# Two more blocks of a fused DeltaNet and hard-swish MLP kernel with fewer multiplications: block one's product with w_out by seven, block three's product with w_in by eleven

## The chip, the cores and the metric

The kernel runs on one core of one Trainium2 chip. The core has five engines that run side by side, each with its own queue of instructions which it takes strictly in order: TensorE (PE in the profile; its weight loads are listed as PEld), VectorE (DVE), ScalarE (ACT), GpSimd (POOL) and SyncE (SP), which here issues nearly all DMAs. An instruction waits at the head of its queue until the semaphores that it names are reached, and everything behind it on that engine waits with it.

The metric is the device time of one execution in microseconds (us). Lower is better.

## The reference

The first half is a gated delta rule over 768 steps for 4 batches and 8 heads of width 48; the second half is a two-layer MLP on the result.

```python
k_n = k / (np.linalg.norm(k, axis=-1, keepdims=True) + 1e-06)
for t in range(S):                                   # 768 steps
    y[:, :, t] = q_t @ state
    v_old = state . k_t
    state += beta_t * outer(k_t, v_t - v_old)
x = y.transpose(0, 2, 1, 3).reshape(3072, 384)
h = x @ w_in                                         # 384 -> 2048
g = h * clip(h + 3, 0, 6) / 6
out = g @ w_out                                      # 2048 -> 384
```

All arrays are float32 but the two weights, which arrive as float64; they are loaded in 16 pieces of 768 KB and converted to float32 on the core.

## The kernel before, in words

**Attention in steps.** The 768 positions are cut into 24 steps of 32. One step t handles 32 positions of all four batches, so 128 rows. Three parts belong to a step:

- its *preparation* (`prep`): GpSimd scales the keys into `kb` (L510), TensorE transposes keys and queries (`pt`, L524), ScalarE copies them to `KQ` (L532), TensorE multiplies them (`sc`, L547), and VectorE masks the products into `L` and `LB` (L558), with masks `mb` that GpSimd makes (L486) and into which only one buffer is given, so a mask waits until VectorE has read the one before. GpSimd also makes `bkb` (L498);
- the *inverse* of the triangular matrices, taken for a group of four steps at once by VectorE in some 60 small instructions with two operands in SBUF (`pr`, `A`: L759, L764), between two large transposes (L469, L473);
- the *chain* of the step, which carries the state: `ks` (L806), `R` (L901, L909), `pz` (L827), `R` from `pz` (L927), `su` (L938), the state's update (L956), `py` (L827), `y` (L819, L863) and the transposition `yt` (L873, L877), which delivers 128 rows of the MLP's input.

Before the preparation of a group, the norms of its keys are needed (`norms`, L409 the square, L413 its sum, L417 to L431 the root and its inverse). For later groups GpSimd does the square, into one buffer, so that squares and sums take turns.

**MLP in blocks.** Two steps make one block of 256 rows, twelve blocks in all. For a block the kernel first makes g = act(x @ w_in) in 16 or 8 portions (*up*) and then g @ w_out (*down*). Both come in a plain form and in one with fewer multiplications:

- `up`: 16 portions of 3 products each, 128x256 (L994), then ScalarE (L1001) and VectorE (L1004);
- `up_by_eleven`: 8 portions, each with 7 products of 128 columns and 2 of 256 columns instead of 6 of 256 (L1066); it wants sums of the weights (`weight_sums`, 16 instructions of GpSimd, L1030), sums of the inputs (`token_sums`, VectorE, L1056), two additions of GpSimd on each portion (L1030) and more of ScalarE (L1080, L1100, L1110) and VectorE (L1093, L1097, L1113);
- `down`: 32 products of 384 columns (L1162), results copied by ScalarE (L1173);
- `down_by_seven`: Strassen's scheme in Winograd's form, 7 products of half width, that is 56 of 192 columns (L1226). Its operands are quarters of w_out (B11, B12, B21, B22) and differences of them (T1, T2, T4, and a last one that replaces B12), made by `quarters` and `last_quarter` (L1197, L1203); sums of g are made by VectorE (L1212) and sums of the results by GpSimd or VectorE (L1236).

Before the change, `FIRST = 2` means that blocks 2 to 11 go down by seven and blocks 0 and 1 plainly, and `UF = 4` means that blocks 4 to 11 go up by eleven and blocks 0 to 3 plainly.

**What sets the order.** The program up to step 5 is written out by hand as a string of words, `ORDER` (L21 and following), in which a word stands for one small piece: `k`, `q`, `v`, `w` for loads, `a` and `c` for the conversion of the weights (L356 on ScalarE; L378, L383, L389 on VectorE), `p9` for the next piece of step 9's preparation, `i2` for the next piece of group 2's inverse, `u` for the next unit of the MLP, and so on. From step 5 on a loop places the work: each step has 15 units; in each unit a piece of the chain or of a preparation is given out by a table (`plan`), one unit of the MLP follows, and pieces of the next group's inverse (`fill`) are added by a budget. Before the change steps 5 and 6 each carry two preparations (`behind`), and group 3's inverse begins at the start of step 7. The pieces of `rest` (conversions, then `quarters`) are given out one in a unit.

The buffers in PSUM are few: a ring of four banks (`pm`) holds `ph`, `po`, `pt`, `pz`, `py` and `yt`; a ring of two double banks (`pc`) holds `sc`, `ks` and `su`. A product of TensorE whose bank still has to be read by VectorE or ScalarE waits for that reader.

The functions that the change touches, with their callers:

Of the kernel before, what the change touches and what calls it, by code (L numbers as in the profile page):

```python
# [36 lines left out]
u h4 k*2 c q k*9 q u p8*2 x4 k ru k*2 gu k c n9 q u q*2 p8 k*2 b7 n9*2 i2 u x4 q i2*2 q ub ru gu u  # L37
rb gb i2*2 h4*2 u*2 i2 ru i2*6 y4 i2 gu i2*7 u i2 ru gu i2 u*3 ru i2*4 gu ru i2*2 v i2 c gu u*3 a u
ru c i2 u*2 i2 gu i2*3 q i2*5 y4 h4 n9 i2 e*2 n9*2 i2*4 q i2 y4 e n9 u ru i2*3 u i2 ru*2 gu h4 u n9
i2*2 u i2 e i2*6 y4 u k n9*3 u gu i2 y4 n9 i2 p9 q i2*2 gu  # L40
# [4 lines left out]
def kernel(  # L45
# [972 lines left out]
    UF = 4  # L1018
# [134 lines left out]
    def down(blk, c, f0):  # L1153
# [7 lines left out]
        for f in range(f0, f0 + WF):  # L1161
            nc.tensor.matmul(  # L1162
                pos[c][:], lhsT=gs[blk, f // 2][:, f % 2, c * P : (c + 1) * P], rhs=w_out[:, f, :],
                start=(f == 0), stop=(f == NFC - 1),
            )
        if f0 + WF == NFC:
# [19 lines left out]
    FIRST = 2  # L1186
# [6 lines left out]
    def quarters():  # L1193

        for o, a, b in ((T1, B12, B11), (T2, B22, T1), (T4, T2, B21)):
            for f in range(0, HF, 2):
                nc.vector.tensor_tensor(  # L1197
# [3 lines left out]

    def last_quarter(f):
        nc.vector.tensor_tensor(  # L1203
            out=B12[:, f : f + 2], in0=B22[:, f : f + 2], in1=B12[:, f : f + 2], op=ALU.subtract
        )

    def down_by_seven(blk):
# [32 lines left out]
        settle()  # L1240
# [56 lines left out]
    def mlp_units():  # L1297
# [21 lines left out]
        for blk in range(1, N // CB):  # L1319
# [82 lines left out]
    def early_norms(t):  # L1402
# [5 lines left out]
    rest = chained(convert(), quarters())  # L1408
    gens.update(
        a=scales(), c=rest, w=pieces(), q=queries(), v=values(), B=betas(), k=keys(), z=settings(), s=more_settings(),  # L1410
# [41 lines left out]
    with tc.manual_schedule():  # L1452
# [111 lines left out]
```

## Time and profile before

| | us |
|---|---|
| median of three executions | 664.48 (664.38 to 665.51) |
| the profiled execution | 662.4 |
| its span in the profile | 660.6 |
| TensorE busy | 633.3 |
| VectorE busy | 492.7 |
| ScalarE busy | 276.7 |
| GpSimd busy | 217.0 |

The profiled execution took 662.4 us, 1.8 us more than its span of 660.6 us. The profile gives the busy time of each engine, the chain of work that ended last, groups of equal instructions by line, and a timeline in which neighbouring instructions of one kind are merged into one row (start, duration, engine, line, operands, shape, count and, in brackets, idle time before it with its releaser). One float32 product of TensorE shows as two records, so a count of x16 stands for eight products. The granted TensorE clock was 0.982 of full speed on average; the stretches below full speed lie in the first 50 us.

The steps can be told from the rows of `ks` (L806) in the chain: step 5 starts at 152.66 us, step 6 at 179.95, step 7 at 207.31, step 8 at 232.91, step 9 at 258.71, step 10 at 283.92.

### The profile page before, as it was taken

What the parts mean: (1) busy time and instruction counts of PE and PEld (TensorE: products, weight loads), DVE (VectorE), ACT (ScalarE), POOL (GpSimd) and SP (SyncE); (2) the same over time, 40 slices, a digit from 0 to 9 for tenths busy, and PEclk for the clock granted to TensorE, in tenths of its full rate; (3) what the DMA queues carried; (4) which work ended last, traced back from release to release, by engine and by line L of the source; (5) the groups of instructions that cost most, each with busy time, mean ns of one, the idle gap of its engine ahead of it and who ended that gap; (6) DMA issues with size and microseconds to landing.
All of it is one profiled execution on the core that took longest, in us unless ns stands there. A gap on an engine that the chain in (4) does not pass through costs nothing.

```text
span 660.6 us, 26484 instructions
## 1 busy us (share of the span) xinstructions
PE 633.3 (96%) x11592; PEld 567.8 (86%) x11592; DVE 492.7 (75%) x1158; ACT 276.7 (42%) x540; POOL 217.0 (33%) x336
## 2 busy tenths in 40 slices
PE   2768999999999999999999999999999999999997
PEld 2657987776789989999999999999999999999997
DVE  5899877798546698758988848989658998456354
ACT  5897689331243142154144244244244144153250
POOL 6531122003411363553254354164052241331430
PEclk9759999999999999999999999999999999999999
DMA  7888246212140030032030030030020020010000
GB/s 178 209 230 201 76 102 164 45 27 42 27 85 3 12 65 3 2 74 38 2 75 2 3 74 2 3 63 3 2 50 2 2 50 2 14 27 1 26 1 24
DMA packets 88691, 33.27 MB, mean 50 GB/s; under 512 B 80224, under 2 KB 83424, under 8 KB 88576
## 3 DMA queue, kind: packets, MB, share of 16 engines
q1 hardware_dynamic: 88224, 31.29, 21.1%
q8 instruction: 91, 1.49, 0.9%
q10 hardware_dynamic: 352, 0.30, 0.2%
q14 instruction: 24, 0.20, 0.1%
HBM read 26.84 MB, written 4.72 MB: 48 GB/s over the span
## 4 chain that ended last, share of the span: by engine, by line
PE 92%; ACT 3%; DVE 2%; DMA 2%; SPq 1%; issue 0%; ACTq 0%; DVEq 0%
PE po L1226 28%; PE ph L1066 24%; PE ph L994 12%; PE po L1162 6%; PE ks L806 4%; PE pt L524 3%; PE py L827 3%; PE pz L827 3%; PE sc L547 3%; PE su L938 3%; ACT spare L356 2%; DMA kf<-in_k_dram 1%; PE yt L873 1%; PE pi L684 1%; DVE pr L730 1%; DVE A L735 0%
## 5 line engine op out<-in xcount | busy, mean ns | idle before, releaser
L1066 PE MATMUL ph<-xT,w_in 128*128 128x128 f32 (+1 forms) x640 | 139.0, 321 | 0.0
L1226 PE MATMUL po<-w_out,g 128*128 128x192 f32 x640 | 110.6, 326 | 0.0
L1066 PEld LDWEIGHTS ph<-xT,w_in 128*128 128x128 f32 x640 | 104.0, 191 | 5.9
L1030 POOL TENSOR_TENSOR g<-g 128x256 f32<-128x256 f32 (+1 forms) x128 | 78.3, 613 | 92.8 <-ACT g L1080 87.8
L1226 PEld LDWEIGHTS po<-w_out,g 128*128 128x128 f32 x640 | 104.6, 190 | 0.5
L994 PE MATMUL ph<-xT,w_in 128*128 128x256 f32 (+1 forms) x480 | 93.3, 343 | 1.5 <-DVE g L1004 1.0
L1226 PE MATMUL po<-spare,g 128*128 128x192 f32 x480 | 86.7, 332 | 0.0
L994 PEld LDWEIGHTS ph<-xT,w_in 128*128 128x128 f32 x480 | 76.2, 190 | 11.5 <-DVE g L1004 1.3
L1226 PEld LDWEIGHTS po<-spare,g 128*128 128x128 f32 x480 | 77.2, 190 | 1.8
L1080 ACT ACTIVATE g<-ph 128x512 f32<-128x512 f32 x64 | 38.2, 597 | 92.8 <-PE ph L1066 92.8
L1236 POOL TENSOR_TENSOR o<-o,u 128x192 f32<-128x192 f32 x18 | 13.7, 762 | 165.9 <-ACT o L1233 87.9
L759 DVE TENSOR_TENSOR pr<-A 128x30 f32<-128x30 f32 (+9 forms) x150 | 58.8, 392 | 3.1
L1093 DVE TENSOR_TENSOR g<-ph,g 128x256 f32<-128x256 f32 x64 | 26.8, 419 | 44.4 <-PE ph L1066 39.5
L1212 DVE TENSOR_TENSOR g<-g 128x512 f32<-128x512 f32 x80 | 56.3, 724 | 4.6 <-PE po L1226 4.5
L764 DVE TENSOR_TENSOR A<-A,pr 128x30 f32<-128x30 f32 (+9 forms) x150 | 56.0, 373 | 3.5
L1001 ACT ACTIVATE g<-ph,halves 128x256 f32<-128x256 f32 (+1 forms) x80 | 33.7, 428 | 56.7 <-PE ph L994 56.7
L356 ACT ACTIVATE spare<-spare,places 128x768 uint16<-128x768 uint16 (+1 forms) x56 | 52.5, 942 | 2.3 <-DMA kf<-in_k_dram 1.2
L1113 DVE SCALAR_TENSOR_TENSOR g<-o,g 128x512 f32<-128x512 f32 x64 | 46.4, 725 | 6.8 <-ACT o L1110 6.8
L1110 ACT ACTIVATE o<-g,halves 128x512 f32<-128x512 f32 x64 | 46.2, 723 | 10.5 <-DVE g L1113 7.8
L1066 PE MATMUL ph<-beta_tok,sums_in 128*128 128x128 f32 x256 | 49.5, 275 | 0.0
L1233 ACT ACTIVATE o<-po 128x192 f32<-128x192 f32 x40 | 13.2, 330 | 82.9 <-PE po L1226 79.3
L510 POOL TENSOR_TENSOR kb<-kf,inv 128x384 f32<-128x384 f32 x24 | 21.7, 905 | 74.0 <-issue 43.1
(141 smaller groups left out, 1022.0 us busy)
## 6 DMA issues: line engine op xcount, KB each, us to landing
kf<-in_k_dram SPq DMA_DIRECT2D x96, 48.0 KB, 2.5
qb<-in_q_dram SPq DMA_DIRECT2D x96, 48.0 KB, 2.7
vf<-in_v_dram SPq DMA_DIRECT2D x96, 48.0 KB, 2.0
out_dram<-o SPq DMA_DIRECT2D x90, 48.0 KB, 1.6
spare<-in_moe_w_in_dram SPq DMA_DIRECT2D x4, 768.0 KB, 5.3
w_out<-in_moe_w_in_dram SPq DMA_DIRECT2D x4, 768.0 KB, 5.6
w_out<-in_moe_w_out_dram SPq DMA_DIRECT2D x4, 768.0 KB, 7.4
spare<-in_moe_w_out_dram SPq DMA_DIRECT2D x4, 768.0 KB, 5.0
```

What stands on the lines that cost most here:

```text
L356: nc.scalar.activation(out=z, in_=z if n else d.bitcast(I16)[:, :, :, 3], func=func, bias=places[:, n : n + 1], scale=scale,)
L759: nc.vector.tensor_tensor(out=pv, in0=A[:, j + 1 :, j].unsqueeze(2).to_broadcast([n, w, j]), in1=A[:, j, 0:j].unsqueeze(1).to_broadcast([n ...
L764: nc.vector.tensor_tensor(out=A[:, j + 1 :, 0:j], in0=A[:, j + 1 :, 0:j], in1=pv, op=ALU.subtract)
L827: nc.tensor.matmul(ps[rows(place(b)), D * h : D * h + D], lhsT=m(h)[rows(b)], rhs=z[rows(b), D * at(h) : D * at(h) + D], start=True, stop= ...
L994: nc.tensor.matmul(ph[:, cols], lhsT=w_in[:, s, f * 128 : (f + 1) * 128], rhs=xT[:, s, cols], start=(s == 0), stop=(s == NKT - 1),)
L1030: nc.gpsimd.tensor_tensor(out=out, in0=a, in1=b, op=op)
L1066: nc.tensor.matmul(ph[:, n], lhsT=w, rhs=x, start=start, stop=stop, skip_group_check=True)
L1110: nc.scalar.activation(out=r, in_=g, func=ACTF.Relu, bias=half, scale=1.0 / 6.0)
L1113: nc.vector.scalar_tensor_tensor(out=g, in0=r, scalar=1.0, in1=g, op0=ALU.min, op1=ALU.mult)
L1162: nc.tensor.matmul(pos[c][:], lhsT=gs[blk, f // 2][:, f % 2, c * P : (c + 1) * P], rhs=w_out[:, f, :], start=(f == 0), stop=(f == NFC - 1),)
L1212: nc.vector.tensor_tensor(out=A(f, *out, 4), in0=A(f, *a, 4), in1=A(f, *b, 4), op=op)
L1226: nc.tensor.matmul(ps[n][:], lhsT=A(f - f % 2, *a)[:, f % 2], rhs=b[:, f], start=(f == 0), stop=(f == HF - 1),)
```

## The change

Block 1 goes down by seven (`FIRST = 1`), and block 3 goes up by eleven (`UF = 3`). So that the operands for block 1 are there in time, `quarters` now makes all four sets of differences, on GpSimd instead of VectorE, as 16 instructions (12 for T1, T2 and T4, 4 for the new B12) which the new words `t` place in `ORDER`: twelve after `b7`, four later. `last_quarter` and the place in `up(2)` that called it are gone, and the MLP's units no longer drain `rest` there. Since T2 and T4 need all of w_out, the last pieces of its conversion (two words `c`, one word `a`) come earlier, ahead of group 2's inverse. `ORDER` has two units `u` less at its end, because block 1's down now has 14 units instead of 16; the loop from step 5 on is thus at the same unit of the MLP as before.

In the loop, step 5 alone is `behind` and carries the preparations of steps 9, 10 and 11 (pieces in units 1 to 6, then 3 to 8, then 9 to 13), and the first piece of step 12's at its end. Step 6 has one preparation as all later steps, and group 3's inverse begins in unit 6 of step 6. The sums of w_in for the products by eleven are made in block 2's down instead of block 3's.

```diff
@@ ORDER
-u h4 k*2 c q k*9 q u p8*2 x4 k ru k*2 gu k c n9 q u q*2 p8 k*2 b7 n9*2 i2 u x4 q i2*2 q ub ru gu u
-rb gb i2*2 h4*2 u*2 i2 ru i2*6 y4 i2 gu i2*7 u i2 ru gu i2 u*3 ru i2*4 gu ru i2*2 v i2 c gu u*3 a u
-ru c i2 u*2 i2 gu i2*3 q i2*5 y4 h4 n9 i2 e*2 n9*2 i2*4 q i2 y4 e n9 u ru i2*3 u i2 ru*2 gu h4 u n9
-i2*2 u i2 e i2*6 y4 u k n9*3 u gu i2 y4 n9 i2 p9 q i2*2 gu
+u h4 k*2 c*3 q k*9 q u p8 a p8 x4 k ru k*2 gu c k n9 q u q*2 p8 k*2 b7 t*12 n9*2 i2 u x4 q i2*2 q ub
+ru gu u rb gb i2*2 h4*2 u*2 i2 ru i2*6 y4 i2 gu i2*7 u i2 ru gu i2 u*3 ru i2*4 gu ru i2*2 v i2 gu
+u*3 t*4 u ru i2 u*2 i2 gu i2*3 q i2*5 y4 h4 n9 i2 e*2 n9*2 i2*4 q i2 y4 e*2 n9 u ru i2*3 u i2 ru*2
+gu h4 u n9 i2*2 u i2*7 y4 k n9*3 gu i2 y4 n9 i2 p9 q i2*2 gu
...
-    UF = 4
+    UF = 3
...
-    FIRST = 2
+    FIRST = 1
...
     def quarters():
-        for o, a, b in ((T1, B12, B11), (T2, B22, T1), (T4, T2, B21)):
+        low = tuple(("low", c, f) for c in range(CB) for f in range(0, HF, WF))
+        for o, a, b, which in (
+            (T1, B12, B11, 14), (T2, B22, T1, 15), (T4, T2, B21, None), (B12, B22, B12, None)
+        ):
+            if which is None:
+                needs(("w", NW - 1), *(low if o is B12 else ()))
+            else:
+                needs(("seen", which, 0), ("seen", which, 1))
             for f in range(0, HF, 2):
-                nc.vector.tensor_tensor(
+                needs(("w", NWI + f // 2))
+                if o is not T1:
+                    needs(("w", NWI + (HF + f) // 2))
+                nc.gpsimd.tensor_tensor(
                     out=o[:, f : f + 2], in0=a[:, f : f + 2], in1=b[:, f : f + 2], op=ALU.subtract
                 )
                 yield
-
-    def last_quarter(f):
-        nc.vector.tensor_tensor(
-            out=B12[:, f : f + 2], in0=B22[:, f : f + 2], in1=B12[:, f : f + 2], op=ALU.subtract
-        )
...
-        settle()
+        if blk > FIRST:
+            settle()
...
-                for n, _ in enumerate((up_by_eleven if blk + 1 >= UF else up)(blk + 1)):
-                    if blk + 1 == FIRST and n >= HF:
-                        drain(rest)
-                        if n % 2:
-                            last_quarter(n - HF - 1)
-                    yield
+                yield from (up_by_eleven if blk + 1 >= UF else up)(blk + 1)
...
-            behind = t - LS < LA - LE
-            first_of = t + min(LA, LE + t - LS)
-            now, more, later = (prep_of(first_of + n) for n in range(3))
+            behind = t == LS
+            now, more, third, later = (prep_of(t + LA - n) for n in (2, 1, 0, -1))
             if not behind:
-                more, later = (), more
+                now = third
...
-                for u in (7, 8, 10, 11, 12, 13):
-                    plan[u] = lambda ch=plan.get(u): (ch and u < 13 and ch(), take(more))
-                plan[14] = lambda: take(later)
-            ready = (2, 0) if behind or i == 2 and t - LS == LA - LE else (1, 6)
+                plan[13] = None
+                for u, gen in zip((3, 5, 6, 7, 8, 9, 10, 11, 12, 13), (more,) * 5 + (third,) * 5):
+                    plan[u] = lambda old=plan.get(u), gen=gen, first=u == 8: (
+                        first and take(gen), old and old(), first or take(gen)
+                    )
+            ready = (1, 6)
...
+            if behind:
+                take(later)
```

More of the change, by code (lines that the diff above doesn't have):

```diff
@@ L1165, in down @@
             )
+        past.add(("low", c, f0))
         if f0 + WF == NFC:
@@ L1407 @@
     g_all = mlp.tile([128, NFC, TB], FP32, name="g", bufs=1)
-    rest = chained(convert(), quarters())
+    rest = convert()
     gens.update(
-        a=scales(), c=rest, w=pieces(), q=queries(), v=values(), B=betas(), k=keys(), z=settings(), s=more_settings(),
+        a=scales(), c=rest, w=pieces(), q=queries(), v=values(), B=betas(), k=keys(), z=settings(), s=more_settings(), t=quarters(),
         ua=up(0, 0), ub=up(0, 1), u=mlp_units(),
@@ L1497 @@
             if behind:
-                for u in (7, 8, 10, 11, 12, 13):
-                    plan[u] = lambda ch=plan.get(u): (ch and u < 13 and ch(), take(more))
-                plan[14] = lambda: take(later)
-            ready = (2, 0) if behind or i == 2 and t - LS == LA - LE else (1, 6)
+                plan[13] = None
[4 more added lines that the diff above has]
+            ready = (1, 6)
             for u in range(NU):
-                if u in plan:
+                if plan.get(u):
                     plan[u]()
```

## The prediction

> **What bounds the kernel now.** I read the page first, for the busy shares and the chain that ended last:
>
> ```profile
> PE 633.3 (96%) x11592; PEld 567.8 (86%) x11592; DVE 492.7 (75%) x1158; ACT 276.7 (42%) x540; POOL 217.0 (33%) x336
> PE 92%; ACT 3%; DVE 2%; DMA 2%; SPq 1%; issue 0%; ACTq 0%; DVEq 0%
> ```
>
> TensorE carries 92% of the chain. Busy time by stretches shows it at 10.00 of every 10 us from 70 to 200 us and within 0.04 us of full on to 600, and the waits of TensorE between 93 and 300 us are nil. So any product taken away there is time saved, and any new wait of TensorE is time lost, in full. The chain in order of time prices the products, plain and with fewer multiplications:
>
> ```profile
> 161.58 5.36 PE po L1162 x16
> ...
> 188.89 5.38 PE ph L994 x24
> ...
> 267.67 5.40 PE po L1226 x32
> ...
> 292.52 5.05 PE ph L1066 x36
> ```
>
> These are the four kinds, each for four units of MLP work. Next, who hands TensorE its work between 110 and 175 us, where the change rearranges everything. TensorE's timeline:
>
> ```profile
> 132.25 2.75 PE L994 MATMUL ph<-xT,w_in 128*128 128x256 f32 x12
> ...
> 147.01 2.74 PE L1162 MATMUL po<-w_out,g 128*128 128x384 f32 x8
> ...
> 155.07 0.60 PE L524 MATMUL pt<-ident,kb 128*128 128x128 f32 x4
> ...
> 160.72 0.86 PE L547 MATMUL sc<-KQ 64*32 64x64 f32 x64
> ...
> 166.87 0.89 PE L938 MATMUL su<-R,bkb 32*64 32x48 f32 x64
> ```
>
> VectorE's and GpSimd's timelines:
>
> ```profile
> 110.10 1.47 DVE L389 SCALAR_TENSOR_TENSOR w_out<-spare 128x768 f32<-128x768 f32 x1
> ...
> 120.59 0.42 DVE L1004 SCALAR_TENSOR_TENSOR g<-g,ph 128x256 f32<-128x256 f32 x1 [1.26 <-ACT g L1001]
> ...
> 132.67 0.41 DVE L1004 SCALAR_TENSOR_TENSOR g<-g,ph 128x256 f32<-128x256 f32 x1
> ...
> 134.27 0.40 DVE L764 TENSOR_TENSOR A<-A,pr 128x228 f32<-128x228 f32 x1
> ...
> 139.43 0.42 DVE L1004 SCALAR_TENSOR_TENSOR g<-g,ph 128x256 f32<-128x256 f32 x1
> ...
> 153.35 0.34 DVE L431 RECIPROCAL inv<-nt 128x32 f32<-128x32 f32 x1
> ...
> 235.14 0.81 DVE L764 TENSOR_TENSOR A<-A,pr 128x228 f32<-128x228 f32 x1
> ```
>
> ```profile
> 108.42 2.33 POOL L498 TENSOR_TENSOR bkb<-kb,beta_tok 128x384 f32<-128x384 f32 x2
> ...
> 153.83 0.83 POOL L510 TENSOR_TENSOR kb<-kf,inv 128x384 f32<-128x384 f32 x1 [43.08 <-issue]
> ...
> 271.28 1.20 POOL L409 TENSOR_TENSOR sq<-kf 128x384 f32<-128x384 f32 x1 [0.67 <-DVE ss L413]
> 273.15 1.20 POOL L409 TENSOR_TENSOR sq<-kf 128x384 f32<-128x384 f32 x1 [0.66 <-DVE ss L413]
> ```
>
> The reader is to see three things. VectorE has no idle time between 121 and 154 us: it works at group 2's inverse and TensorE lives on a margin of tenths. The same instruction (L764, 228 elements) takes 0.40 us with GpSimd still and 0.81 us while GpSimd works. And GpSimd's idle 43 us before 153.83, where the new differences go, is the very time in which VectorE has none.
>
> **What is saved.** *Down of block 1:* its nine pieces of L1162 in the chain sum to 21.24 us; block 2's seven pieces by seven (L1226, the same steps' interruptions) sum to 18.80. Saved: 2.4 us. *Up of block 3:* 21.32 us (L994, from 229 us) against 20.07 for block 4 (L1066): 1.3 us; steps 7 and 8 together last 51.4 us, steps 9 and 10 50.0, which agrees. Together -3.7 us, all on the path.
>
> **What is hidden.** The twelve quarter sums leave VectorE in step 5 (0.54 to 0.85 us each) and the eight sums of block 1 (L1212, 0.68 free) come in; TensorE waited for neither. The last four (L1203) leave up(2). The 16 sums of w_in move one block earlier on GpSimd; in steps 8 and 9 of before they ran beside the plain up(3) and an inverse with no wait of TensorE, and they meet the same there now; without that cover each would cost its 0.8 us. Block 3's extra work for VectorE (token sums 2.0 us a block, L1093, L1097, L1113 11.5 against 6.6) and ScalarE (12.8 against 6.8) meets an inverse that starts nine units sooner, as in steps 10 to 12, which keep TensorE full. SyncE's loads keep their places; the outputs of block 1 now wait for the end of its product, as every later block's do. Preparation 11 moves from step 6 to 5 with all its instructions: the same 1.7 us of TensorE (two `pt` of 0.43, one `sc` of 0.8), elsewhere.
>
> **Wait C: VectorE falls behind under the new differences.** In its queue the last conversion (L383, L389: 2 x 0.95 us) now stands before the inverse. 1.26 us of it fit in the idle time before 120.59; with that the queue is 0.6 us late. GpSimd may start T2 when that L383 ends, near 120.9, and then has T2, T4 and the new B12 back to back: twelve instructions of 128x384, 0.83 us each (L510 free). The first six meet L389 (once, +0.5) and then instructions that read PSUM or one operand, which the rows show unharmed (L558 0.41, L413 0.55, L469 1.97 in either case); the other six meet the inverse's first pairs. What does one cost VectorE? The nearest row is the L389 at 110.10 beside the second 128x384 `bkb`: 1.47 against 0.95, +0.52. So 0.6 + 0.5 + 6 x 0.52 = 4.2, less 0.5 for two L1004 that run underneath: 3.7 us late near 133 us. TensorE's second half of the row at 132.25 (from 133.55) needs the bank that the L1004 at 132.67 frees, at 133.08: slack 0.5. TensorE waits about 3.2 us, wherever on the way it comes. Ends: GpSimd's 128x256 sums cost 0.29 each (two rounds of the inverse from 234.19 to 237.56 last 3.37 instead of 2.18, beside four of them), giving 1.8 us; 0.83 each, full exclusion, gives 5.1. I take 0.52 since that row has instructions of the same size. A gain is excluded, since TensorE waits for nothing there today.
>
> [...]
>
> **Wait D: the keys of step 9 come too late.** After 139 us VectorE works without a gap from the L1004 at 139.43, which follows TensorE's own portion, to the reciprocal at 153.35, whose result `kb` needs (L510, 153.83 to 154.66). None of that gets shorter; the conversions left before 139.43. TensorE's `pt` is at 155.07, 0.4 later. But between 147.01 and that `pt` TensorE now has three half products by seven (24 records, 3.9 us) instead of 20 plain records (6.6 us): it arrives 2.7 us sooner and waits 2.3. C shifts both alike. Ends: 0.4 if VectorE could use the 1.9 us of the conversions, 2.7 if `kb` also slips.
>
> **Wait E: three preparations in step 5.** `sc` of step 10 now stands three units after step 9's, before `su`, and `su` needs its second double bank back: VectorE must have made `LB` of step 10. In VectorE's queue that L558 stands behind three sums L413 of the norms, each waiting for a GpSimd square. GpSimd's queue holds, before the first square, step 10's mask, which waits for step 9's `LB`. From the end of step 9's `sc`: `LB` +0.8, two masks 1.2 to 1.6, one addition 0.6 to 0.8, then three rounds of square and sum at 1.87 (271.28 to 273.15) less a little for the first, L558 twice 0.75: about 9. TensorE gets there after four half products (5.2), two transposes (0.9) and `sc` (0.8): 6.9. Wait 2.0; ends 0.5 (squares at 0.83 free) and 2.6.
>
> **Sum.** -3.7 + 3.2 + 2.3 + 2.0 = +3.8 us. Against the profiled execution of 662.4 us (span 660.6 and 1.8 around it, which stay): 666.2. That execution lies 2.1 us under the median of the three, 664.48; on that median the sum gives 668.3.
>
> **Rivals.** *Full exclusion* (condition: each of the six differences costs VectorE its 0.83): C is 5.1, the sum +5.7, 670.2 us. *E does not bite* (GpSimd's squares free of VectorE's sums, so the rounds take 1.4): E 0.5, sum +2.3, 666.8 us. For it: in step 5 of before squares followed at 1.8 to 2.5 us, not faster, so little. [...]
>
> **How the numbers follow.** Main case 0.55, full exclusion 0.13, no E 0.17, ahead 0.10, a mixture within the bound 0.05. What a measurement of this kernel can tell from no change is 0.2%, 1.3 us. The first three are slower by more: 0.85; faster 0.10; same 0.05. The low ends of C, D and E together give -1.0 us (663.5), the high ends +6.7 (671.2). The range, 663.2 to 671.2, holds these and leaves out the faster case.
>
> **What would show it.** L1162 halves to 64 records; block 1's L1226 lasts 18.8 us. TensorE's waits, nil now between 93 and 300 us, show VectorE's L1004 near 130 to 137, GpSimd's `kb` at step 5's first `pt`, and VectorE's L558 at step 5's `su`. L759 and L764 right after L469 show 0.5 to 0.9 us instead of 0.2. From step 7 on every step lasts 25 us. If the waits are not there, I am wrong in the queues; if they are and the sum differs, in a price.

## The result, and the profile after

The changed kernel is slower: 674.5 us (median of six executions, 670.3 to 677.6) against 664.2 us for the kernel before on the same chip, a ratio of 1.0146 with a 95% interval of 1.0105 to 1.0188. Measured again it was 675.5 us, ratio 1.0137 (1.0097 to 1.0177). The forecast was 668.3 us. Its sign holds, its size does not: +3.8 us were forecast, about +10 came, and the time lies above the range.

The page of the changed kernel, busy shares and then the chain that ended last:

```profile
PE 631.5 (94%) x11688; PEld 575.3 (86%) x11688; DVE 502.6 (75%) x1164; ACT 282.2 (42%) x551; POOL 243.7 (36%) x373
...
PE 83%; issue 6%; DVE 4%; DMA 3%; POOL 2%; ACT 1%; SPq 1%; POOLq 0%; DVEq 0%
```

TensorE is busy for 1.8 us less than before, in a span that is 11.5 us longer (672.1 against 660.6; the execution took 673.81 us). Its share of the chain fell from 92% to 83%, and "issue", time for which the profile shows no releaser, rose from 0% to 6%. Most of that 6% is no wait of TensorE: 25.7 us of it are GpSimd's idle time from the end of its last difference (136.67 us) to the next `kb` (162.44), along which the chain is followed. What TensorE itself lost is in its timeline. It shows the new waits, in brackets with their releaser; before the change there was none from 93 to 300 us:

```profile
130.35 0.88 PE L827 MATMUL pz<-R,X 32*32 32x48 f32 x64 [1.00 <-DVE g L1004]
...
138.76 1.56 PE L994 MATMUL ph<-xT,w_in 128*128 128x256 f32 x6 [2.15 <-DVE g L1004]
142.09 1.56 PE L994 MATMUL ph<-xT,w_in 128*128 128x256 f32 x6 [1.77 <-DVE g L1004]
...
163.36 0.66 PE L524 MATMUL pt<-ident,kb 128*128 128x128 f32 x4 [2.04 <-POOL kb L510]
...
178.93 0.84 PE L938 MATMUL su<-R,bkb 32*64 32x48 f32 x60 [1.47 <-DVE LB L558]
...
277.51 0.30 PE L547 MATMUL sc<-KQ 64*32 64x64 f32 x2 [0.96 <-issue]
...
479.44 1.78 PE L1232 MATMUL po<-spare,g 128*128 128x192 f32 x10 [0.87 <-issue]
```

The first three are wait C (4.9 us together), then D (2.0) and E (1.5), in the places that the prediction named. The last two were in no step of it. VectorE and GpSimd under C:

```profile
120.12 0.74 DVE L901 SCALAR_TENSOR_TENSOR R<-ks,parity,vf 128x192 f32<-128x192 f32 x2 [1.72 <-ACT y L843]
...
129.05 0.94 DVE L764 TENSOR_TENSOR A<-A,pr 128x30 f32<-128x30 f32 x1
...
130.99 0.92 DVE L764 TENSOR_TENSOR A<-A,pr 128x58 f32<-128x58 f32 x1
131.94 0.94 DVE L759 TENSOR_TENSOR pr<-A 128x84 f32<-128x84 f32 x1
132.92 0.93 DVE L764 TENSOR_TENSOR A<-A,pr 128x84 f32<-128x84 f32 x1
...
136.85 0.29 DVE L764 TENSOR_TENSOR A<-A,pr 128x130 f32<-128x130 f32 x1
```

```profile
116.94 3.88 POOL L1208 TENSOR_TENSOR spare<-w_out 128x384 f32<-128x384 f32 x4 [3.06 <-ACT spare L356]
124.27 4.71 POOL L1208 TENSOR_TENSOR spare<-w_out,spare 128x384 f32<-128x384 f32 x4 [3.45 <-DVE spare L383]
128.93 3.85 POOL L1208 TENSOR_TENSOR spare<-spare,w_out 128x384 f32<-128x384 f32 x4
132.75 3.92 POOL L1208 TENSOR_TENSOR w_out<-w_out 128x384 f32<-128x384 f32 x4
```

While GpSimd worked here, VectorE finished one two-operand instruction for each of GpSimd's: GpSimd's came every 0.96 us, and six of VectorE's, of 30 to 108 elements, lasted 0.92 to 0.95. From 136.85 on, with GpSimd still, 130 elements took 0.29. The pace was GpSimd's own: its four differences from 116.94 on came at the same distance (3.88 us for four), although VectorE was idle among them for 1.72 us, up to 120.12. So in this stretch VectorE alone was held up; only the first difference, at 124.27, had itself waited, beside an L389 of VectorE.

The kernel before shows the same one for one where GpSimd makes sums of w_in beside an inverse. Each of VectorE's instructions ends 0.25 us after one of GpSimd's:

```profile
236.20 0.59 DVE L759 TENSOR_TENSOR pr<-A 128x234 f32<-128x234 f32 x1
236.83 0.81 DVE L764 TENSOR_TENSOR A<-A,pr 128x234 f32<-128x234 f32 x1
```

```profile
235.66 0.88 POOL L1030 TENSOR_TENSOR w_in<-w_in 128x256 f32<-128x256 f32 x1
236.49 0.89 POOL L1030 TENSOR_TENSOR sums_in<-w_in 128x256 f32<-128x256 f32 x1
```

Where the time went is read from the length of the steps, from one first `ks` (L806) to the next. Step 5 has one preparation more in the changed loop (1.66 us) and step 6 one less.

| us | step 4 | 5 | 6 | 7 | 8 | 9 | 17 | start of step 4 | from there to the last step |
|---|---|---|---|---|---|---|---|---|---|
| before | 37.30 | 27.29 | 27.36 | 25.60 | 25.80 | 25.21 | 25.09 | 115.3 | 484.9 |
| after | 40.27 | 33.31 | 25.54 | 25.09 | 24.92 | 26.33 | 26.12 | 118.4 | 492.7 |
| after, second profile | 42.28 | 36.61 | 25.54 | 25.39 | 24.93 | 25.08 | 25.84 | 116.7 | 496.7 |

The start of step 4 varies by chance: where the early steps were left alone it came between 115.3 us (the profile of before, the earliest) and 120.3 us in the profiles below, with and without the change. The last column is free of it: +7.7 us in one execution of the changed kernel and +11.8 in another.

### The profile page after: what moved, and what is told of

Same layout as the page of the kernel before. It is cut to its first block, busy times and chain, and to the rows that moved or that the text cites. A ratio compares the mean times of both kernels' runs of the same rounds, so it can differ in the third digit from the quotient of the medians.

```text
span 672.1 us, 26761 instructions
## 1 busy us (share of the span) xinstructions
PE 631.5 (94%) x11688; PEld 575.3 (86%) x11688; DVE 502.6 (75%) x1164; ACT 282.2 (42%) x551; POOL 243.7 (36%) x373
## 4 chain that ended last, share of the span: by engine, by line
PE 83%; issue 6%; DVE 4%; DMA 3%; POOL 2%; ACT 1%; SPq 1%; POOLq 0%; DVEq 0%
PE po L1232 29%; PE ph L1066 27%; PE ph L994 7%; PE ks L806 3%; PE su L938 3%; PE pz L827 3%; PE py L827 3%; PE pt L524 3%; PE sc L547 2%; PE po L1162 1%; PE yt L873 1%; DMA w_out<-in_moe_w_in_dram 1%; DMA kf<-in_k_dram 1%; POOL spare L1208 1%; PE pi L684 1%
## 5 line engine op out<-in xcount | busy, mean ns | idle before, releaser
L1066 PE MATMUL ph<-xT,w_in 128*128 128x128 f32 (+1 forms) x720 | 156.5, 321 | 0.0
L1030 POOL TENSOR_TENSOR g<-g 128x256 f32<-128x256 f32 (+1 forms) x144 | 88.3, 614 | 104.6 <-ACT g L1080 99.0
L1232 PE MATMUL po<-w_out,g 128*128 128x192 f32 x704 | 122.1, 326 | 0.0
L1232 PEld LDWEIGHTS po<-w_out,g 128*128 128x128 f32 x704 | 115.0, 190 | 0.7
L1232 PE MATMUL po<-spare,g 128*128 128x192 f32 x528 | 95.8, 332 | 0.9 <-issue 0.9
L1232 PEld LDWEIGHTS po<-spare,g 128*128 128x128 f32 x528 | 84.9, 190 | 3.0 <-issue 1.0
L994 PE MATMUL ph<-xT,w_in 128*128 128x128 f32 (+1 forms) x384 | 72.5, 338 | 4.7 <-DVE g L1004 3.9
L994 PEld LDWEIGHTS ph<-xT,w_in 128*128 128x128 f32 x384 | 59.4, 194 | 12.7 <-DVE g L1004 4.9
L764 DVE TENSOR_TENSOR A<-A,pr 128x30 f32<-128x30 f32 (+9 forms) x150 | 57.6, 384 | 3.3
L1113 DVE SCALAR_TENSOR_TENSOR g<-o,g 128x512 f32<-128x512 f32 x72 | 52.6, 730 | 7.6 <-ACT o L1110 7.6
L1066 PE MATMUL ph<-beta_tok,sums_in 128*128 128x128 f32 x288 | 55.7, 275 | 0.0
L1001 ACT ACTIVATE g<-ph,halves 128x128 f32<-128x128 f32 (+1 forms) x64 | 26.2, 418 | 45.4 <-PE ph L994 45.4
L1066 PEld LDWEIGHTS ph<-beta_tok,sums_in 128*128 128x128 f32 x288 | 43.7, 192 | 0.0
```

Source lines behind the costliest of these rows:

```text
L764: nc.vector.tensor_tensor(out=A[:, j + 1 :, 0:j], in0=A[:, j + 1 :, 0:j], in1=pv, op=ALU.subtract)
L994: nc.tensor.matmul(ph[:, cols], lhsT=w_in[:, s, f * 128 : (f + 1) * 128], rhs=xT[:, s, cols], start=(s == 0), stop=(s == NKT - 1),)
L1030: nc.gpsimd.tensor_tensor(out=out, in0=a, in1=b, op=op)
L1066: nc.tensor.matmul(ph[:, n], lhsT=w, rhs=x, start=start, stop=stop, skip_group_check=True)
L1113: nc.vector.scalar_tensor_tensor(out=g, in0=r, scalar=1.0, in1=g, op0=ALU.min, op1=ALU.mult)
L1232: nc.tensor.matmul(ps[n][:], lhsT=A(f - f % 2, *a)[:, f % 2], rhs=b[:, f], start=(f == 0), stop=(f == HF - 1),)
```

## The experiments

Each was compared with the kernel before on the same chip. In the kernels that add lines ahead of it a line of the code can be one higher (L928 is L927 there).

**One wait at a time.** Four variants of the changed kernel. *Small sums* (`e1`) cuts GpSimd's differences to 2 of 192 columns and lets the products by seven read B11 in place of T1, T2 and T4. It thus leaves out most of the differences and doesn't compute the reference's result; it serves to time the rest:

```diff
-out=o[:, f : f + 2], in0=a[:, f : f + 2], in1=b[:, f : f + 2]
+out=o[:, f : f + 2, 0:2], in0=a[:, f : f + 2, 0:2], in1=b[:, f : f + 2, 0:2]
-product(4, A22, T4, 0)
+product(4, A22, B11, 0)
...
```

> The changed kernel with its sixteen GpSimd differences cut to 2 of 192 columns, and the products that would read T1, T2 and T4 reading B11 instead (left out: most of the quarter differences, so the last factor of the MLP is not the reference's). Theory 'three waits': the GpSimd differences alone make wait C, so the three waits of TensorE on VectorE's L1004 between 128 and 143 us (1.00, 2.15 and 1.77 us in the changed kernel, 4.9 together) vanish and the time falls by 4.9 us, from 674.5 to about 669.6; the inverse's L759 and L764 right after L469 take 0.13 to 0.35 us instead of 0.92 to 0.97. Rival for C: the two conversions moved ahead of the inverse (1.9 us of VectorE) do it, then 1.4 to 2 us of waits are left there and the time falls by only about 3. Rival 'program': the rest of the loss (the start-up, 3 us later at step 4 than in the profile of before, and two waits without a releaser, 0.96 us in step 9 and 0.87 us at 479 us) belongs to the new program, then step 4 starts near 118 us here too; if it is chance, it starts near 115.5 us in some of these kernels.

Measured: 668.1 us, ratio 1.0044 (1.0027 to 1.0061). The waits of C are gone, and step 4 lasts 35.07 us instead of 40.27: C costs 5.2 us. VectorE behind L469:

```profile
126.19 0.21 DVE L764 TENSOR_TENSOR A<-A,pr 128x30 f32<-128x30 f32 x1
...
127.09 0.22 DVE L764 TENSOR_TENSOR A<-A,pr 128x58 f32<-128x58 f32 x1
...
127.62 0.25 DVE L764 TENSOR_TENSOR A<-A,pr 128x84 f32<-128x84 f32 x1
```

The eight instructions of the inverse that were long sum to 7.13 us in the changed kernel and to 1.97 here: 5.2 us, all of C, 0.65 us for each of the eight differences beside them. The conversions that were moved ahead cost nothing that can be seen. The time fell by 1.0% of 664 us, that is 6.8 us, known to some 3 us, which agrees with 5.2. D, E and the `sc` wait of step 9 (1.22 us) stayed.

*Keys early* (`e2`):

```diff
-gu h4 u n9 i2*2 u i2*7 y4 k n9*3 gu i2 y4 n9 i2 p9 q i2*2 gu
+gu h4 u n9 i2*2 n9*3 u n9 p9 i2*7 y4 k gu i2 y4 i2 q i2*2 gu
```

> The changed kernel with the last four pieces of the norms of step 9's group (L420, L422, L426, L431) and the key scaling of step 9 (L510) put ahead of the inverse's last nine pieces. Theory 'three waits': the reciprocal L431 comes near 160 us instead of 162.4, the wait of TensorE's first pt of step 5 on L510 (2.04 us) goes to nil and the time falls by 2.0 us, to about 672.5. Rival: VectorE is itself the limit there, the wait moves on to pz of step 5 (the inverse's last piece L473 comes 1 us later), and the time falls by less than 1 us.

Measured: 676.8 us, ratio 1.0181 (1.0155 to 1.0207): nothing gained, where 2.0 us had been expected. VectorE in this kernel, then TensorE, then the clock:

```profile
158.77 0.35 DVE L431 RECIPROCAL inv<-nt 128x32 f32<-128x32 f32 x1
...
159.30 0.88 DVE L764 TENSOR_TENSOR A<-A,pr 128x130 f32<-128x130 f32 x1
160.21 0.57 DVE L759 TENSOR_TENSOR pr<-A 128x108 f32<-128x108 f32 x1
...
163.13 0.41 DVE L1004 SCALAR_TENSOR_TENSOR g<-g,ph 128x256 f32<-128x256 f32 x1
```

```profile
163.69 0.63 PE L524 MATMUL pt<-ident,kb 128*128 128x128 f32 x4 [3.17 <-DVE A L764]
```

```profile
160.00:164.00 4.00, 0.83 (x7) 1.00 0.14 25
164.00:168.00 4.00, 4.00 (x19) 0.60 0.00 0
```

(In the last, a stretch, its length, TensorE's busy time, the granted clock.) GpSimd has the keys ready at 160.0 us and `pt` still starts at 163.69. The profile now names VectorE; what `pt` still needs from it is a bank, which the L1004 at 163.13 frees, behind the inverse: TensorE's semaphore instruction for it stands at 163.58, just behind the end of that L1004 (163.54) and before that of the L764 named (163.67). And GpSimd's work of the preparation, now beside that inverse, makes it slower: the five instructions from 159.30 take 3.5 us instead of 1.3. So the rival is right that VectorE's queue is the limit, and not the place of the keys alone; but the wait did not move to `pz`, it stayed at `pt` and grew by 1.1 us, and half clock came behind it and behind `su`. No experiment took D away.

*Squares later* (`e3`):

```diff
-take(fill, 2 if i or u < 2 else u > 4)
+take(fill, 2 if i or u < 2 else u > 4 and not behind)
```

> The changed kernel with the four squares and sums of norms (L409, L413) of step 5 moved to step 6. Theory 'three waits': L558 of step 10 follows its sc at once, the wait of su in step 5 (1.47 us) goes to nil and the time falls by 1.5 us, to about 673.0. Rival: the squares do not make that wait (the masks do), then su waits 1 us or more here too; or the squares bring a like wait to step 6, and the time stays at 674.5.

Measured: 671.7 us, ratio 1.0096 (1.0068 to 1.0123). L558 of step 10 follows its product,

```profile
175.39 0.42 DVE L558 TENSOR_TENSOR L<-sc,mb 128x256 f32<-128x256 f32 x1 [2.37 <-PE sc L547]
```

`su` does not wait, and step 5 lasts 31.57 us instead of 33.31. E is the squares, as predicted, and costs 1.7 us; no like wait came in step 6.

*All three* (`e4`) has these edits in one kernel, and leaves out what `e1` leaves out.

> The edits of the three kernels before in one (small GpSimd differences, with most of the quarter differences left out and B11 read for T1, T2 and T4; keys early; squares in step 6). Theory 'three waits': no wait of TensorE on VectorE or GpSimd over 0.3 us is left between 128 and 185 us; from ks of step 4 to ks of step 9 it takes 149.1 - 4.9 - 2.0 - 1.5 = 140.7 us (143.35 before, so 2.6 less, and the 3.7 us saved by the products less 1.1 us that I cannot place). If start-up and the waits without a releaser are chance, the time is 660.5 to 662.5 us, 2 to 4 under the kernel before; if they belong to the new program, 666 us, 2 over it.

Measured: 668.0 us, ratio 1.0045 (1.0026 to 1.0064), no better than the small sums alone. The early keys make `pt` wait 3.18 us here as well, and the clock behind it is 0.50 for 3.41 us; that uses up what E gave back. Both expected times are missed, since both took D to be gone.

**The parts alone.** *Block one by seven* (`e7`) is the changed kernel with `UF = 4` and the loop of before; *block three by eleven* (`e6`) is one number in the kernel before:

```diff
-    UF = 4
+    UF = 3
```

> The changed kernel with block three plain and the loop as before (two preparations in steps 5 and 6), so block one by seven with the GpSimd differences alone. Theory 'three waits': the saving is in step 4 (two units less, 2.4 us), C costs 5.2 and D 2.0 as in the changed kernel, E is gone: 664.5 - 2.4 + 5.2 + 2.0 = 669.3 us, and step 5 waits once, at pt (2.0 us). Rival: E comes from the units by seven with their sums L1218 rather than from the third preparation; then su of step 5 or 6 waits 1 us or more here too and the time is near 671.

> The kernel before with block three's product with w_in by eleven and nothing else (block one's product with w_out as before, the loop as before with two preparations in steps 5 and 6). Theory: -1.3 us, in steps 7 and 8 (51.4 us before, 50.0 to 50.1 here), and none of the waits C, D, E: 663.4 to 663.9 us. A stretch of TensorE's instructions moves against the blocks of 256, so a wait of up to 1 us may come or go. Rival: the loop had to be changed for it, since the inverse of group 3 begins only in step 7 and VectorE has 7 us more to do in steps 7 and 8; then pz of step 9 waits 1 us or more and the gain is gone.

By seven alone: 672.3 us, ratio 1.0100 (1.0069 to 1.0131). TensorE waits for C and at `pt` (2.03 us), not at `su`, so E needs the changed loop with its third preparation; step 4 lasts 42.23 us, not 40.3, for a reason that follows. By eleven alone: 669.7 us, ratio 1.0056 (1.0038 to 1.0074), the rival: with the old loop group 3's inverse is late. TensorE:

```profile
245.39 0.38 PE L1066 MATMUL ph<-xT,w_in 128*128 128x128 f32 x2 [1.21 <-issue]
...
272.36 1.50 PE L827 MATMUL pz<-R,X 32*32 32x48 f32 x64 [2.48 <-DVE X L473]
```

With the changed loop and block one as before (`e10`; `e9` also has the squares in step 6):

> The same with the squares where the changed kernel has them (step 5). Theory 'E': su of step 5 waits 1.4 to 1.8 us for L558 of step 10 here too, and the time is that of the kernel with the squares in step 6 plus 1.5 to 3.2 us (the wait, and perhaps a stretch of half clock behind it). Rival: without block one's units by seven VectorE comes to L558 sooner or later than in the changed kernel, and the two differ by less than 0.7 us.

> The kernel before with block three by eleven, the changed loop (three preparations in step 5, one in step 6, group 3's inverse from step 6) and the squares of step 5 moved to step 6; block one as before. Theory: steps 7 and 8 save 1.3 us, the inverse of group 3 is in time (no wait at pz of step 9, 2.48 us with the old loop), no C, D or E: 664.2 to 665.2 less 1.3, that is 663 to 664 us, if no block of instructions stalls. Rival: in step 5 VectorE has the twelve quarter differences (0.54 to 1.02 us each) as well as three preparations; L558 of step 10 or 11 is late, TensorE waits 1 us or more at su or ks, and the time is 665 to 667.

`e10`: 665.8 us, ratio 1.0006 (0.9986 to 1.0026). `e9`: 667.3 us, ratio 1.0033 (1.0010 to 1.0057). Both expected times are missed: `e9` was to take 663 to 664 us, and `e10` was to be slower than `e9` by 1.5 us or more. The wait at `pz` is gone. In `e10` `su` waits only 0.56 us, so E in full needs block one's work by seven as well (VectorE has differences in place of block one's sums there, which is probably why). What eats the 1.3 us in `e10` are 0.9 us in steps 5 and 6 (55.6 against 54.65), that 0.56 among them, and once more a wait without a releaser:

```profile
245.40 0.49 PE L1066 MATMUL ph<-xT,w_in 128*128 128x128 f32 x2 [1.38 <-issue]
```

In `e9` there are two (1.53 us at L994 near 196 us, 0.56 near 247), so it could not show what the squares are worth.

**Is it the exclusion?** `e8` does the same differences on VectorE (`nc.vector` for `nc.gpsimd` in `quarters`).

> The changed kernel with the sixteen quarter differences on VectorE at the same places of the program. Free, one takes VectorE 0.55 us (0.54 to 1.02 in the kernel before), 8.8 us in all. Theory 'full exclusion': a GpSimd difference costs VectorE 0.65 to 0.7 us where it meets a two-operand instruction, as much as if VectorE did it itself, so the twelve that met work cost the same here, and only the first four (T1, at 117 us, which met little) come on top: the time changes by 0 to +3 us, 674.5 to 677.5. Rival 'a part only': a GpSimd difference costs VectorE 0.3 to 0.5, as I priced it; then the move adds 16 x 0.55 - 12 x 0.4 = 4 us or more, 678.5 or over.

Measured: 676.0 us, ratio 1.0145 (1.0103 to 1.0187), 0.5 to 1.5 us over the two times of the changed kernel: within the bounds of full exclusion, but the intervals are some 5 us wide. The step says more: with half clock in both, step 4 lasts 43.25 us against 42.28 in the changed kernel's second profile, 1.0 more, where the other theory asked for 4. VectorE and TensorE in this kernel:

```profile
127.91 1.96 DVE L1208 TENSOR_TENSOR spare<-w_out,spare 128x384 f32<-128x384 f32 x4
129.79 1.96 DVE L1208 TENSOR_TENSOR spare<-spare,w_out 128x384 f32<-128x384 f32 x4
```

```profile
134.87 1.50 PE L827 MATMUL pz<-R,X 32*32 32x48 f32 x64 [5.75 <-DVE g L1004]
```

VectorE needs 0.49 us for a difference. Leaving it to GpSimd cost VectorE 0.65 for each of the eight that met the inverse, and nothing that can be seen for the other eight.

**What a wait costs beyond its length.** The changed kernel a second time:

> The changed kernel itself a second time. Theory 'waits and clock': the waits of TensorE are those of its first profile to 0.3 us (4.9 us under VectorE's L1004 near 130 to 142, 2.0 at pt, 1.5 at su, about 0.9 each at sc of step 9 and near 479 us), since they are in the program. What may differ are stretches of half clock (0.50, 3.41 or 6.83 us long) behind these waits, as in three of the variants; each makes the step that it falls in 1.7 to 2 us longer (step 4 42.2 instead of 40.3, step 5 35 instead of 33.3). That explains times between 670 and 678 us. Rival: the spread comes from the start-up alone (ks of step 4 between 115 and 120 us); then steps 4 and 5 last 40.3 and 33.3 us here too and the clock after 60 us is 1.00 throughout.

Measured: 675.5 us, ratio 1.0137. Stretches of the changed kernel (busy TensorE, granted clock in the last column but two), first profile and second:

```profile
136.00:146.00 10.00, 6.08 (x22) 1.00 0.00 1
...
164.00:170.00 6.00, 6.00 (x158) 1.00 0.01 3
...
180.00:188.00 8.00, 8.00 (x164) 1.00 0.06 16
```

```profile
136.00:146.00 10.00, 8.03 (x19) 0.66 0.00 1
...
164.00:170.00 6.00, 6.00 (x31) 0.72 0.00 0
...
180.00:188.00 8.00, 7.11 (x150) 0.79 0.01 2
```

The same waits (1.01, 2.16, 0.92, 2.03, 1.48 us; the third was 1.77 in the first profile) are followed by a clock of 0.50 in the second profile, for 6.83 us from 137.6, 3.41 from 164.9 and 3.41 from 182.0, and by none in the first. Step 4 lasts 2.0 us longer for it and step 5 3.3. The program is the same, so this is chance: over the profiles, the 2.03 us at `pt` were followed by half clock in three of seven, the 1.48 us at `su` in three of six, C in four of seven. The three stretches start whole multiples of 3.41 us apart (27.3 and 17.1 us, 8 and 5 times), and so do those of the start-up in the first profile (from 15.22, 32.29 and 52.77 us, 5 and 6 times). Why half clock came behind these waits in one profile and not in the other is not shown.

To see it apart from GpSimd, `e11` makes waits in the kernel before:

```diff
+        for _ in range({10: 18, 12: 20, 14: 22, 16: 24, 18: 26, 20: 30}.get(t, 1)):
             nc.scalar.activation(out=Zt[:], in_=pz[:, 0:DM], func=ACTF.Copy)
```

> The kernel before with ScalarE's copy of pz into R (L927) issued 18, 20, 22, 24, 26 and 30 times instead of once in steps 10, 12, 14, 16, 18 and 20 (0.35 to 0.49 us each, the same result), so that TensorE waits in the middle of a stretch in which it never waited; nothing else is changed, and GpSimd has no part in it. It measures what a wait costs beyond its length. [...] I expect waits of 0 to 1 us for 18 copies and 4 to 6 us for 30, at least two stretches of half clock, and a sum of extra step time above the sum of waits by 1.7 us for each. [...]

Measured: 732.4 us. TensorE waited 6.07, 7.11, 8.05, 9.20, 11.03 and 13.12 us (a copy more costs 0.59 us, not 0.35 to 0.49), all longer than I wanted, so this run says nothing of 2 us. The six steps grew by 8.91, 9.11, 10.66, 11.08, 13.21 and 15.08 us: by the wait and another 1.9 to 2.8, with half clock at each. The first:

```profile
303.83 0.80 PE L1067 MATMUL ph<-xT,w_in 128*128 128x128 f32 x2 [6.07 <-ACT R L928]
```

```profile
300.00:309.30 9.30, 5.47 (x51) 0.63 0.34 58
```

**The waits without a releaser.** All that are 0.3 us or longer and come after 60 us, 38 in the 18 profiles, are at the same place: if all of TensorE's instructions in the trace (weight loads, products and some 190 semaphore instructions) are counted from the start of the program, from 0, the first late one has a number that leaves 193 on division by 256. And each wait ends 2.2 to 3.0 us after a packet of 16 KB of the instruction queue. That queue moved 91 or 92 such packets in every run, about one for each 256 of the 23,370 to 23,625 instructions; in the profile of before no two of them start closer than 3.33 us. In the changed kernel, the stretch ahead of the one at 277.51:

```profile
275.00:275.50 0.50, 0.50 (x56) 1.00 0.13 33
275.50:276.50 1.00, 1.00 (x89) 1.00 0.00 0
276.50:277.50 1.00, 0.04 (x3) 1.00 0.00 0
```

The packet moves in the first row; TensorE runs through the short products of `pz` and `sc` (64 records and as many weight loads in 0.8 us) and stops two records before the end of `sc`. My reading is a block of 256 instructions that was used up before the next was there; the trace shows the packet, the count and the stop, not the cause. `e5` moves the count by 56:

```diff
-            of_heads(py, lambda b: b ^ 1, lambda h: LB[:, he(h), :], Z)
+            of_heads(py, lambda b: b ^ 1, lambda h: LB[:, he(h), :], Z, again=14 if t == 7 else 0)
```

> The changed kernel with 14 products of py of step 7 issued a second time into the same place, 56 more instructions of TensorE, which cost it 14 x 0.026 = 0.4 us and change no result. The waits of TensorE without a releaser in the changed kernel and its variants (sc in step 9, 0.92 to 1.22 us; L1232 near 479 us, 0.39 to 0.87) all lie at instruction 193 modulo 256 of TensorE's stream, 2.3 to 2.6 us after the DMA queue of the instructions took up a block. Theory 'block of instructions': TensorE has run out of instructions, because a burst of short products emptied a block before the next one was there. In the kernel before TensorE has 199 instructions less at step 9, so 56 more (255 in all) put the blocks back to where they lie there, and both waits go: step 9 lasts 25.1 to 25.3 us instead of 26.3, step 17 25.1 instead of 26.1, the time falls by 2.0 - 0.4 = 1.6 us. Rival: the waits come from a semaphore that the profile does not show; then they stay in sc of step 9 and at 479 us, 0.9 us each, and the time rises by 0.4 us.

Steps 9 and 17 last 25.09 us each: both waits are gone. The time is 676.0 us all the same, ratio 1.0153 (1.0119 to 1.0188), as this execution had half clock behind C, D and E (steps 4 and 5 as in the second profile). Another 0.4 us came in step 15. The second profile of the unshifted kernel has no wait in step 9 either (25.08 us), so the surer of the two is the wait near 479 us: the seven other profiles of the changed kernel and of its variants with both parts all have it, and `e5` has not. (The wait of step 9 is in four of the seven.) `e13` does the opposite, 100 instructions more in the kernel before (`again=25 if t == 1`):

> The kernel before with 25 products of py of step 1 issued a second time and nothing else, 100 more instructions of TensorE (0.6 us at most, in the start-up). By the count of the profile of before it is among the worst places: fifteen blocks after 60 us would pass in under 3.4 us instead of five. Theory 'block of instructions': waits without a releaser appear in a kernel that has none, at the blocks near 158, 194, 221, 398, 441, 520, 543, 566 and 588 us or some of them, 0.4 to 1.5 us each, 3 to 6 us in sum, and the time rises to 1.005 to 1.009 of the kernel before. Rival: the waits belong to the rearranged work, not to the count; then there are none after 100 us and the time is 1.000 to 1.001.

Measured: 673.5 us, ratio 1.0120 (1.0099 to 1.0141). Who TensorE waited for from 70 to 200 us (of before: nobody):

```profile
PE sc L547 <- issue: 3.6, 2, 3.2
PE su L939 <- issue: 1.2, 1, 1.2
PE pi L684 <- issue: 0.4, 1, 0.4
```

Twenty-five tiny products, 0.6 us of work, cost 8 to 9 us (at most 6 had been expected), by waits of up to 3.16 us and half clock behind the longest. So the count alone makes such waits, in a kernel that has no other change. Where they come I had wrong: they are in steps 1 to 3, and of the places that I listed only the one near 441 us (454 here) shows something, a step longer by 0.3 us. At most of the other borders, the places of that remainder in the count, the packet had come earlier (12.5 us ahead at the border near 274 us of the changed kernel, the one before its wait at 277.51), and a block that was run through quickly was not always followed by a wait (in before one took 2.20 us from 373.1 us on, and TensorE did not stop).

Three tries to put `e10` on a better count:

> The kernel before with block three by eleven and the changed loop, squares in step 5 (the kernel that came out at 1.0006 of the time before), and 33 products of py of step 1 issued a second time, 132 more instructions of TensorE ahead of everything that matters (0.9 us at most, in the start-up, where TensorE often waits). In its profile blocks of 256 instructions, counted from instruction 193, that TensorE ran through in under 3.3 us after 176 us fell short by 8.7 us in sum; with the count moved by 132 by 1.0 us. Theory 'block of instructions': the wait of 1.38 us at L1066 near 245 us goes, steps 5 to 9 take 130.5 us instead of 132.1, and the time falls by 1.5 us, to 664.2, that is 0.998 of the kernel before. Rival: the wait has another cause and stays at the first L1066 of step 8, and the time rises by up to 0.9 us.

> The kernel before with block three by eleven and the changed loop, squares in step 5, and 33 products of pz of step 5 issued a second time (132 instructions, 0.86 us), behind the early steps, which the same number placed in step 1 had made 9 us longer. Of the 0.86 us some 0.5 are hidden under the wait of su in step 5 (0.56 us). Theory 'block of instructions': steps 1 to 4 are as without it, the wait of 1.38 us near 245 us goes, as it did there, step 8 lasts 24.9 us, and the time is 665.8 - 1.7 + 0.3 = 664.4 us, 0.998 of the kernel before. Rival: another block falls short between 165 and 300 us, and the time stays at 1.000 to 1.002.

> The same with 17 products (68 instructions, 0.44 us, all of it under the wait of su): by the count two or three blocks fall short, by 2.3 us in sum instead of 1.0. Theory: the wait near 245 us goes, one of 0.2 to 0.6 us comes elsewhere, and the time is within 0.5 us of the version with 33 products. Rival: as there.

`e12`: 673.2 us, ratio 1.0124 (1.0101 to 1.0147). Step 8 lasts 24.92 us, the wait near 245 us is gone as expected, but the early steps, where products are shortest, got five new ones. `e14`: 666.1 us, ratio 1.0022 (1.0006 to 1.0038): step 8 is right (24.93 us), and 1.34 us came back in step 5, at the first border behind the added products. `e15`: 666.9 us, ratio 1.0029 (1.0012 to 1.0047): 1.91 us near 352 us, with half clock. All three missed the expected 664.2 to 664.9 us: the count moved the wait near 245 us away each time, and others came. No version that beats the kernel before was found; `e10` equals it.

## Why the prediction was right or wrong

The sum, by its own terms, beside the two profiles (from the start of step 4 to the last step):

| us | predicted | first profile | second | from |
|---|---|---|---|---|
| saved | -3.7 | -3.6 | -3.3 | step 4 of `e1` 35.07 against 37.30; steps 7 and 8, 50.01 and 50.32 against 51.40 |
| C | 3.2 | 5.2 | 5.2 | step 4, `e1` |
| D | 2.3 | 2.0 | 2.0 | wait at `pt` |
| E | 2.0 | 1.7 | 1.7 | step 5, `e3` |
| steps 5 and 6, not placed | 0 | 0.4 | 0.4 | 58.85 against 54.65, less D and E |
| waits without a releaser | 0 | 2.1 | 0.6 | steps 9 and 17 against those of before |
| half clock | 0 | 0 | 5.3 | steps 4 and 5, second less first |
| sum | 3.8 | 7.8 | 11.9 | measured 7.7 and 11.8 |

- *What bounds the kernel, the savings, the hidden work*: right. Both savings came to within 0.2 us in the first profile, and steps 7 and 8 show no price for the sums of w_in, the work of block three or the moved preparation.
- *Wait C*: the mechanism was right (`e1`), and so was the start: "near 120.9" is 5.6 us behind the start of step 4 before the change, and T2 started 5.9 us behind it (124.27 against 118.4). The size was off by both factors. "0.83 us each (L510 free)": a difference takes GpSimd 0.96 us, and the first, beside the L389 at 124.28, took 1.8, so four of the twelve were done when the inverse began, not six, and eight met it. "I take 0.52": each cost VectorE 0.65, because VectorE got through one instruction for each of GpSimd's; what that cost followed from how short VectorE's own were, and those at the start of the inverse are the shortest (0.2 to 0.3 us). The row at 110.10 was one long instruction that met one, and the 0.29 of the sums of w_in came from longer ones (0.40), with the same one for one. 8 x 0.65 is 5.2. Of the 0.6, 0.5 and -0.5 around it, the 0.6 was there (the inverse began 0.66 us later in its step, also in `e1`, where TensorE doesn't wait, so the slack took it); the L389 was not longer (0.95). *Full exclusion*, the rival with 0.13, is nearer to what the chip did, but its 5.1 us came out right by luck: six at 0.83, where it was eight at 0.65. An instruction of 30 elements took 0.94 us beside a difference, and 0.21 without one (`e1`).
- *Wait D*: right to 0.3 us, and at the right place. That it can be had back by moving the keys was my error of the next step (`e2`).
- *Wait E*: right in its cause (`e3`, `e7`), though block one's work by seven has a part in it (`e10`). The rounds took 1.87 us as worked out, and `LB` came 8.8 us after `sc` (predicted 9); TensorE took 7.5 us to `su`, not 6.9, hence 1.5 of wait.
- *"From step 7 on every step lasts 25 us"*: true of steps 7 and 8, not of 9 and 17. No term of the sum stood for TensorE's own instructions, whose count the change moves by 199.
- *The step that failed* is the sum: "any new wait of TensorE is time lost, in full" was taken to mean C, D and E at their own length and nothing else. One of its terms was mis-sized, C with 3.2 for 5.2. Two were put at nothing without a reason. One is TensorE's waits without a releaser: they took 2.1 us in the first profile and 0.6 in the second. The other is the clock: waits of 1.5 to 2.2 us brought half clock behind them in about half of the profiles, up to 1.7 us for each 3.41, which made 5.3 us in the second profile and none in the first. Half clock is also a part of why the times of the changed kernel reach from 670 to 678 us; another part is the start-up, with which those of the kernel before reach from 662 to 670 over all its runs.
- *The other rivals* fell: E did bite (1.7 us), and VectorE was behind, not ahead.
- *The range* ended at 671.2 because its high end added the high ends of C, D and E alone. With C at 5.2 the waits give +5.7, that is 670.2 us, still inside it; the other 2 to 6 us, the two terms above, took the time out of it.

Not settled: the 0.4 us of steps 5 and 6, and the share of half clock in the mean, which two profiles can't give; the start of step 4 came on average 1 us later in the nine profiles of the changed kernel and its variants than in seven of before and its own, against a spread of 5 us, so a small part of the 10 us may lie there.

## What to carry to other kernels

On an engine that was never idle, price a new wait above its length: here half clock, for 3.41 us, came behind waits of 1.48 and of 2.03 us in three of six and three of seven profiles, and waits that cost 8.9 us in sum cost up to 5.3 us more. Before moving element work to GpSimd, see whether VectorE is in a run of short two-operand instructions at that time: here each of the eight differences that met such a run cost VectorE 0.65 us, more than the 0.49 of doing it itself. Count how many of VectorE's instructions fall under GpSimd's, not how long they are: eight at 0.65 made C's 5.2 us. And when a kernel is full to the tenth, a change of the instruction count is a change of its own (100 instructions, 0.6 us of work, cost 8 to 9 us in `e13`): look for waits without a releaser behind bursts of short products before blaming the edit.

## What had not been expected of the hardware

- TensorE stopped without a releaser at one place in the count of its instructions by 256: 38 waits of 0.30 to 3.16 us, all at the remainder 193, and all ended 2.2 to 3.0 us after a packet of the instruction queue. They came and went with the count and in part with timing (step 9 waited 0.96 us in one profile of the changed kernel and not in the other).
- The granted clock fell to 0.50 for 3.41 us, or multiples of it, behind a wait of 1.48 us and of 2.03 us, in three of six and three of seven cases, and also of 1.84, 1.91 and 2.48 us (`e12`, `e15`, `e6`); and behind all ten waits over 3 us that were seen after the start-up.
- Where VectorE and GpSimd both had instructions with two operands in SBUF (129 to 137 us of the changed kernel), VectorE finished one for each of GpSimd's: 0.96 us for each pair, which was GpSimd's pace alone too, where VectorE's took 0.2 to 0.3 by themselves.
